# First chunk of x by DMA transpose, first product pair ahead of the parameters, exponentials on GpSimd, and a new order of products

## The chip, the cores and the metric

The kernel runs on one core of one Trainium2 chip. Its engines work side by side and meet through semaphores: TensorE (matrix products, PE in the profile), VectorE (DVE), ScalarE (ACT), GpSimd (POOL) and SyncE (SP), which here only issues DMA transfers. ScalarE can issue transfers too. The metric is the device time of one execution in microseconds, lower is better.

## What is computed

The reference mixes two branches of a token sequence x (2048 tokens, 448 columns, bfloat16) by a gate per token. Branch a is a state-space layer with 448 complex states, a recurrence over the tokens; branch b is a feed-forward layer with 1792 hidden columns.

```python
x = A_x
g = sigmoid((x * gate_w).sum(-1, keepdims=True))
# branch a
Lam = Lambda_re + 1j * Lambda_im
dt = exp(log_dt)
Lam_bar = exp(dt * Lam)
B_bar = ((Lam_bar - 1.0) / Lam)[:, None] * (B_re + 1j * B_im)
Bu = einsum("bld,pd->blp", x + 0j, B_bar)
h_t = Lam_bar * h_(t-1) + Bu_t            # for every token t
y = 2.0 * einsum("blp,dp->bld", h, C_re + 1j * C_im).real + x * Dskip
# branch b
b = silu(x @ w1) @ w2
out = g * y + (1 - g) * b
```

## The kernel before

The tokens are cut into 4 chunks of 512. For each chunk there are five kinds of work.

- *B products* (`bu`, line 635): x times the transposed B, seven slots of 128 rows (`BT`), into `U`. Slots 0 to 2 and half of slot 3 are the real part, the rest the imaginary part.
- *Lanes* (`lanes`, line 654): the complex recurrence is turned by cosine and sine tables (`COS`, `SIN`) into real scans. DVE does the turning, seven scans of 512 tokens (line 665), and the turning back into `H`. ScalarE or, for the slots named in `GP` (line 626), GpSimd casts each scan's result from `Gf` to `Gb`. Small GpSimd products carry the state to the next chunk (`k1`, `k2`, `gin`).
- *First FFN product* (`f1`, line 690): x times w1, 14 blocks of 128 hidden columns, evicted by ScalarE with Silu into `aT`.
- *Second FFN product* (`ffn2`, line 697) for each block of 128 tokens: 14 products with w2, evicted by ScalarE with the factor 1 − g into `Tb`.
- *Readout* (`readout`, line 717) for each block of 128 tokens: 7 products of `H` with `CP`, then a DVE instruction that adds the rest, then the store.

`bu` and `f1` need x transposed (`xT`: four column blocks, the last of them columns 320 to 447, of which the half not covered already counts). They are made in pairs by `step` (line 605): a pair is 14 "half steps", products over 64 rows that use the upper and the lower half of the array in turn, 8 that begin the pair and 6 that end it. A pair stays open until the next one has begun; `close` (line 621) ends it at once.

The head of the kernel. SP issues the x load of chunk 0, four B loads, ten w1 loads, the w2 load, and then DMA transposes of x for chunk 1 and of C. ScalarE issues four small parameter loads (`prm`) and loads the table for Exp. TensorE first runs 15 filler products on a zeroed tile (`idle`, line 420), then transposes chunk 0 of x in 16 pieces (`x_transposes`, line 432), the parameters (`prm_t`, line 485) and B slots 0 and 1 (`b_transposes`, line 458). DVE and ScalarE copy the results from PSUM to SBUF. From the transposed parameters `pc` (line 495) ScalarE makes `dtc` = exp(log_dt) and `rc` = exp(dt Re Lambda) (lines 500 and 504), and then loads the table that has Silu and Sin. DVE makes the phases for the tables from `dtc`. GpSimd makes `gwc`, the gate weights, from `pc`; `gates` (line 767) needs them.

The order of work. Each call of `add` puts an operation with its engine, estimated cost and priority into a `Plan`. `order` (line 102) runs a small model: TensorE keeps the order in which the operations were added (the calls at lines 800 to 868), the other queues take at each moment a ready operation with the lowest priority number, and PSUM banks are assigned on the way. What comes out is the fixed order of instructions of each engine. The estimated costs therefore influence the orders and the banks, and nothing else. `Waits` then puts in the semaphore waits.

Of the kernel before, what the change touches and what calls it, by code (L numbers as in the profile page):

```python
# [46 lines left out]
class Plan:  # L47
# [6 lines left out]
    SWITCH = 0.10  # L54

# [46 lines left out]
    def order(self):  # L102
# [28 lines left out]
        while len(done) < len(ops):  # L131
# [20 lines left out]
            if o.sem is not None:  # L152
                free[o.eng] = t + o.cost
                if o.bytes > 4096:
                    pipe = max(pipe, t + 1.5) + o.bytes / 260e3
                    o.end = pipe + 0.4
                else:
                    o.end = t + 3.4
            else:
# [4 lines left out]
                free[o.eng] = o.end = t + o.cost + extra  # L164
# [97 lines left out]
def bass_gated_mix__ssm_conv_s5__dense_activation_silu__prompt_kernel(nc, A_x, A_Lambda_re, A_Lambda_im, A_B_re, A_B_im, A_C_re, A_C_im,  # L262
               A_log_dt, A_Dskip, B_x, B_w1, B_w2, gate_w, out):
    with ExitStack() as ctx:
# [26 lines left out]
        Cnat = Tb[0:112, 13:15, :].rearrange("p a b -> p (a b)")[:, 0:768].rearrange("p (b l) -> p b l", b=4)  # L291
        gwc = sb("gwc", [128, 4], BF16)
# [13 lines left out]
        pc = sb("pc", [128, 4, 4], F32)  # L306
        dtc = sb("dtc", [128, 4], F32)
# [49 lines left out]


# [7 lines left out]
        def load_xt(tc, n, prio, cost, reads=()):  # L366

            rows = slice(tc * CH, (tc + n) * CH)
            for k, (o, c) in enumerate(((slice(0, 3), slice(0, 384)), (slice(3, 4), slice(320, 448)))):
                P.add("sp", lambda e, o=o, c=c: e.dma_start_transpose(xT[:, o, rows], x2[rows, c]), list(reads),  # L370
                      [f"xT{t}{k}" for t in range(tc, tc + n)], cost[k], prio + k, sem(), n * CH * (1100, 500)[k])

        load_x(0, 0)
        load("sp", Bnat[:, 0:3, :], A_B_re[0:384, :].rearrange("(s p) d -> p s d", p=128), "Bn0", 384 * 896, 1)
        load("sp", Bnat[:, 4:7, :], A_B_im[0:384, :].rearrange("(s p) d -> p s d", p=128), "Bn3", 384 * 896, 2)
        load("sp", Bnat[0:64, 3, :], A_B_re[384:448, :], "Bn1", 64 * 896, 3)
        load("sp", Bnat[64:128, 3, :], A_B_im[384:448, :], "Bn2", 64 * 896, 4)
        for h, (c0, c1) in enumerate(((0, 384), (384, 896))):
            w = w1s[:, :, :].rearrange("p b (q f) -> p b q f", q=2)
            for b in range(3):  # L380
                load("sp", w[:, b, :, c0:c1], B_w1[128 * b:128 * b + 128, :].rearrange("p (q f) -> p q f", q=2)[:, :, c0:c1],
                     f"w1{h}{b}", 128 * 4 * (c1 - c0), 5 + h)
            load("sp", w[64:128, 3, :, c0:c1], B_w1[384:448, :].rearrange("p (q f) -> p q f", q=2)[:, :, c0:c1],
                 f"w1{h}3", 64 * 4 * (c1 - c0), 5 + h)
            load("sp", w1s[0:64, 3, c0:c1], B_w1[320:384, c0:c1], f"w1{h}4", 64 * 2 * (c1 - c0), 5 + h)
# [11 lines left out]
        def late_loads():  # L397
# [4 lines left out]
            for tc in range(1, NCH):  # L402
# [12 lines left out]
        ACT(lambda e: e.preload_act_table(AF.Exp), [], ["tbl"], 1.3, 4)  # L415


        DVE(lambda e: e.memset(PB[:, 0, :], 0.0), [], ["PB0"], 0.2, 0)  # L418

        def idle(n):  # L420
# [6 lines left out]
            P.add("pe", mm, ["PB0"], [tk], 0.107 * n)  # L427

        idle(15)


        def x_transposes(h, n):

            tk = Ps()

            def mm(pe):
                for q in range(2):
                    for b in range(2):
                        o = (q * 2 + b) * 128
                        c = XCOL[2 * n + q]  # L440
                        r = pe.transpose(bk16(tk)[:, o:o + 128], xnat[:, 2 * h + b, c:c + 128], ident[:, :])  # L441
                return r
            P.add("pe", mm, ["xn0", "ident"], [tk], 0.24)
            dst = xT[:, 2 * n:2 * n + 2, 256 * h:256 * h + 256]
            src = lambda: bk16(tk)[:, 0:512].rearrange("p (q n) -> p q n", q=2)
            if n == 0:
                DVE(lambda e: e.tensor_copy(dst, src()), [tk], [f"xT00{h}"], 0.42, 0)
            else:
                ACT(lambda e: e.activation(dst, src(), AF.Copy), [tk], [f"xT01{h}"], act_cost(512), 0)

        for h in range(2):
            for n in range(2):
                x_transposes(h, n)

        def xr(tc):
            return [f"xT{tc}{k}" for k in (range(2) if tc else ("00", "01", "10", "11"))]

        def b_transposes(slots, reads, h, to_act):
# [11 lines left out]
            P.add("pe", mm, reads + ["ident"], [tk], 0.06 * 2 * n)  # L470
# [10 lines left out]

        prmn = [f"prm{k}" for k in range(4)]
# [9 lines left out]
        b_transposes(B01, ["Bn0"], 0, False)  # L492
        b_transposes(B01, ["Bn0"], 1, True)
        idle(2)
# [5 lines left out]
        ACT(lambda e: e.activation(dtc[:, :], LDT, AF.Exp), ["pc", "tbl"], ["dtc"], 0.25, 1)  # L500
# [3 lines left out]
        ACT(lambda e: e.activation(rc[:, :], rc[:, :], AF.Exp), ["rc", "tbl"], ["rc"], 0.25, 1)  # L504
        ACT(lambda e: e.preload_act_table_set("silu_and_others"), [], ["tbl", "dtc", "rc"], 1.3, 2)
# [48 lines left out]
        DVE(lambda e: e.tensor_single_scalar(ph[:, 4:8], ph[:, 0:4], 512.0, ALU.mult), ["ph"], ["ph5"], 0.2, 12)  # L554
        DVE(nearest(phk[:, 4:8], ph[:, 4:8]), ["ph5"], ["phk5"], 0.2, 12)
        DVE(minus(ph[:, 4:8], ph[:, 4:8], phk[:, 4:8]), ["ph5", "phk5"], ["ph5"], 0.2, 12)
        ACT(lambda e: e.activation(s8[:, :], ph[:, :], AF.Sin, scale=TURN), ["ph", "ph5", "tbl"], ["s8"], 0.25, 12)
        ACT(lambda e: e.activation(pha[:, :], ph[:, :], AF.Abs), ["ph", "ph5", "tbl"], ["pha"], 0.25, 12)
        ACT(lambda e: e.activation(c8[:, :], pha[:, :], AF.Sin, bias=hpi[:, :], scale=-TURN), ["pha", "hpi", "tbl"], ["c8"], 0.3, 12)
# [344 lines left out]
```

## Time and profile before

| what | us |
|---|---|
| three runs | 143.53, 144.14, 144.27; median 144.14 |
| the profiled execution | 143.92 |
| its span, from first to last instruction | 142.0 |
| TensorE busy | 137.6 (97%) |
| DVE busy | 126.1 (89%) |
| ScalarE busy | 79.1 (56%) |
| GpSimd busy | 34.2 (24%) |

The lines of the profile name a line of the code, an engine, an operation, the tile written and the tiles read (buffer numbers left out), and a count. A busy TensorE is not a TensorE at its peak, as matmuls are pipelined and the ends are modelled. The chain of waits is followed back from the last instruction: at each moment it shows the piece of work that the end waited for. L599 is the half steps, L703 the second FFN product, L731 the readout, L425 the filler, L441 the x transposes, L468 the B transposes, L774 the gates.

### The profile page before, as it was taken

What the parts mean: (1) busy time and instruction counts of PE and PEld (TensorE: products, weight loads), DVE (VectorE), ACT (ScalarE), POOL (GpSimd) and SP (SyncE); (2) the same over time, 40 slices, a digit from 0 to 9 for tenths busy, and PEclk for the clock granted to TensorE, in tenths of its full rate; (3) what the DMA queues carried; (4) which work ended last, traced back from release to release, by engine and by line L of the source; (5) the groups of instructions that cost most, each with busy time, mean ns of one, the idle gap of its engine ahead of it and who ended that gap; (6) DMA issues with size and microseconds to landing.
All of it is one profiled execution on the core that took longest, in us unless ns stands there. A gap on an engine that the chain in (4) does not pass through costs nothing.

```text
span 142.0 us, 2706 instructions
## 1 busy us (share of the span) xinstructions
PE 137.6 (97%) x1069; PEld 70.6 (50%) x1069; DVE 126.1 (89%) x145; ACT 79.1 (56%) x148; POOL 34.2 (24%) x66
## 2 busy tenths in 40 slices
PE   6989999999999999999999999999999999999993
PEld 4855555544444544444555554444455555555552
DVE  0399999998899299999999999999999999899393
ACT  3386698798965494889811014898721355411100
POOL 7184000089009520443450002542000000000000
PEclk9999999999999999999999999999999999999999
DMA  4989969201947600101000102000001021000113
GB/s 133 331 258 290 314 133 201 33 0 39 239 103 188 229 5 0 37 0 42 2 31 1 41 29 69 18 18 5 0 30 34 0 69 37 31 1 32 32 65 99
DMA packets 21108, 11.44 MB, mean 81 GB/s; under 512 B 11492, under 2 KB 21096, under 8 KB 21096
## 3 DMA queue, kind: packets, MB, share of 16 engines
q1 hardware_dynamic: 21088, 11.27, 30.5%
q8 instruction: 8, 0.13, 0.4%
q14 instruction: 4, 0.03, 0.1%
q10 hardware_dynamic: 8, 0.00, 0.0%
HBM read 6.25 MB, written 1.84 MB: 57 GB/s over the span
## 4 chain that ended last, share of the span: by engine, by line
PE 96%; DVE 1%; ACT 1%; POOL 1%; issue 0%
PE ps L599 45%; PE ps L703 30%; PE ps L731 15%; PE ps L425 2%; PE ps L441 1%; PE ps L774 1%; ACT BT L475 1%; PE ps L468 1%; POOL cw L562 0%; DVE ot L735 0%; PE ps L751 0%; DVE PB L418 0%; POOL gwc L497 0%; DVE pc L495 0%; DVE cw L570 0%
## 5 line engine op out<-in xcount | busy, mean ns | idle before, releaser
L599 PE MATMUL ps<-xT,w1s 64*128 64x512 bf16 x392 | 47.4, 376 | 0.0
L703 PE MATMUL ps<-w2s,aT 128*128 128x448 bf16 x224 | 44.7, 352 | 0.0
L692 ACT ACTIVATE aT<-ps 128x512 bf16<-128x512 f32 x56 | 30.0, 601 | 5.3 <-PE ps L599 5.2
L599 PEld LDWEIGHTS ps<-xT,w1s 64*128 64x128 bf16 x392 | 21.0, 94 | 22.7 <-issue 0.7
L703 PEld LDWEIGHTS ps<-w2s,aT 128*128 128x128 bf16 x224 | 21.7, 98 | 20.3 <-issue 0.4
L665 DVE TENSOR_TENSOR_SCAN Gf<-rc,gin,PA 128x512 f32<-128x512 f32 x21 | 26.8, 1322 | 0.0
L599 PE MATMUL ps<-xT,BT 64*128 64x512 bf16 x196 | 25.9, 376 | 0.7 <-DVE ph L511 0.6
L707 ACT ACTIVATE Tb<-ps,g 128x448 bf16<-128x448 f32 x16 | 10.1, 633 | 28.0 <-PE ps L703 21.4
L731 PE MATMUL ps<-CP,H 128*128 128x448 bf16 (+1 forms) x119 | 23.2, 341 | 0.0
L671 ACT ACTIVATE Gb<-Gf 128x512 bf16<-128x512 f32 x24 | 14.7, 630 | 8.4 <-DVE Gf L665 8.3
L599 PEld LDWEIGHTS ps<-xT,BT 64*128 64x128 bf16 x196 | 10.7, 94 | 12.1 <-DVE phk L508 0.8
L731 PEld LDWEIGHTS ps<-CP,H 128*128 128x128 bf16 x119 | 11.5, 98 | 9.8 <-issue 0.4
L633 ACT ACTIVATE U<-ps 128x512 bf16<-128x512 f32 x24 | 13.3, 592 | 2.2 <-PE ps L599 2.2
L735 DVE SCALAR_TENSOR_TENSOR ot<-ps,g,tf 128x448 bf16<-128x448 f32 (+1 forms) x17 | 11.1, 650 | 3.2 <-issue 2.2
L669 POOL CAST Gb<-Gf 128x512 bf16<-128x512 f32 x4 | 6.1, 1518 | 23.0 <-DVE Gf L665 23.0
L721 DVE SCALAR_TENSOR_TENSOR tf<-xnat,g,Tb 128x448 f32<-128x448 bf16 x16 | 10.6, 674 | 0.1
L652 DVE TENSOR_TENSOR PB<-Gb,SIN 128x1536 bf16<-128x1536 bf16 (+1 forms) x8 | 8.6, 1087 | 1.2 <-ACT Gb L671 1.1
L652 DVE TENSOR_TENSOR PB<-U,SIN 128x2048 bf16<-128x2048 bf16 (+1 forms) x8 | 8.6, 1080 | 0.0
L652 DVE TENSOR_TENSOR PA<-U,COS 128x3584 bf16<-128x3584 bf16 x4 | 8.1, 2020 | 0.2
L652 DVE TENSOR_TENSOR PA<-PA,PB 128x3584 bf16<-128x3584 bf16 x4 | 8.1, 2018 | 0.0
L652 DVE TENSOR_TENSOR H<-PA,PB 128x3584 bf16<-128x3584 bf16 x4 | 8.1, 2014 | 0.0
L652 DVE TENSOR_TENSOR PA<-Gb,COS 128x3584 bf16<-128x3584 bf16 x4 | 8.1, 2014 | 0.0
(97 smaller groups left out, 100.5 us busy)
## 6 DMA issues: line engine op xcount, KB each, us to landing
xnat<-in_A_x_dram SPq DMA_DIRECT2D x4, 448.0 KB, 6.1
out_dram<-ot SPq DMA_DIRECT2D x15, 112.0 KB, 1.7
w2s<-in_B_w_dram SPq DMA_DIRECT2D x1, 1568.0 KB, 9.3
w1s<-in_B_w_dram SPq DMA_DIRECT2D x3, 256.0 KB, 4.6
w1s<-in_B_w_dram SPq DMA_DIRECT2D x3, 192.0 KB, 4.3
Gb<-Gb SPq DMA_DIRECT2D x8, 64.0 KB, 1.9
U<-U SPq DMA_DIRECT2D x6, 64.0 KB, 2.0
Tb<-in_A_B_re_dram SPq DMA_DIRECT2D x1, 336.0 KB, 3.7
```

The lines of the kernel that those rows point to most:

```text
L599: r = pe.matmul(bk(tk), w[p0:p0 + 64, k, c0:c0 + 128], xT[p0:p0 + 64, k, xc:xc + CH], start=(start and i == 0), stop=(not start and i == 2))
L633: ACT(lambda e: e.activation(U[:, s, :], bk(tk), AF.Copy), [tk], [f"U{s}"], act_cost(512), 4)
L652: return DVE(lambda e: e.tensor_tensor(o, a, b, op), r, w, dve_cost(n, 2), prio)
L665: DVE(lambda e, s=s, b=b, init=init: e.tensor_tensor_scan(Gf[:, s, :], rc[:, b:b + 1].to_broadcast([128, CH]), PA[:, s, :], init, ALU.mult ...
L669: POOL(lambda e, s=s: e.tensor_copy(Gb[:, s, :], Gf[:, s, :]), [f"Gf{s}"], [f"Gb{s}"], 0.75, 8)
L671: ACT(lambda e, s=s: e.activation(Gb[:, s, :], Gf[:, s, :], AF.Copy), [f"Gf{s}"], [f"Gb{s}"], act_cost(512), 4)
L692: ACT(lambda e: e.activation(aT[tc % 2][:, fb, :], bk(tk), AF.Silu), [tk, "tbl"], [f"aT{tc % 2}_{fb}"], act_cost(512), 3)
L703: r = pe.matmul(bk(tk)[:, 0:D_MOD], aT[tc % 2][:, fb, o:o + 128], w2s[:, fb, :], start=(fb == 0), stop=(fb == NFB - 1))
L707: ACT(lambda e, tk=tk: e.activation(Tb[:, tb, :], bk(tk)[:, 0:D_MOD], AF.Copy, scale=g1[:, tb:tb + 1]), [tk, f"g1_{tc}"], [f"Tb{tb}"] + [f ...
L721: DVE(lambda e: e.scalar_tensor_tensor(tf[tb % 2][:, :], xnat[:, tb, :], g[:, tb:tb + 1], Tb[:, tb, :], ALU.mult, ALU.add), [f"xn{tc}", f" ...
L731: r = pe.matmul(bk(tk)[:, 0:n], Ht[:, s, o:o + 128], CP[:, s, c], start=(s == 0), stop=(s == NSLOT - 1))
L735: DVE(lambda e, tk=tk, c=c, n=n: e.scalar_tensor_tensor(ot[tb % 3][:, c], bk(tk)[:, 0:n], g[:, tb:tb + 1], tf[tb % 2][:, c], ALU.mult, ALU ...
```

## The change

- Chunk 0 of x: columns 0 to 383 come by a DMA transpose on SP's queue, into `xT`. The last column block, 320 to 447, is loaded as it is by ScalarE's queue into the new tile `xlast`, transposed by TensorE in 4 pieces (`xl_t`) and copied by one DVE instruction. The natural copy of chunk 0, needed only for the skip term, is loaded with the late loads, after the first chunk's lanes.
- B_re rows 0 to 255 are loaded by ScalarE's queue ahead of `xlast` and of the four parameter loads; rows 256 to 383 get a load of their own on SP. The w1 loads are 8 instead of 10.
- TensorE's head: 12 filler products instead of 15, B slots 0 and 1, `xl_t`, 2 filler products, the first pair of B products, and only then the parameters, B slots 4 to 6, the end of the first pair, the gates, and B slots 2 and 3.
- `dtc` and `rc` are made by GpSimd as e to a power, with a constant tile `ebase`; ScalarE loads only the table with Silu and Sin.
- The phases of the carried state (`s8`, `c8`) get a higher priority; some casts of `Gb` move to GpSimd (`GP`).
- The order of products of all chunks is changed; the planner has new constants for several operations.

The functions `half_steps`, `step`, `close`, `u_out`, `bu` and `swapped` are only moved ahead of the first pair.

```diff
+    OVERLAP = {"act": 0.10, "dve": 0.08}
...
-                free[o.eng] = o.end = t + o.cost + extra
+                o.end = t + o.cost + extra
+                free[o.eng] = o.end - self.OVERLAP.get(o.eng, 0.0)
...
-        load_x(0, 0)
-        load("sp", Bnat[:, 0:3, :], A_B_re[0:384, :].rearrange("(s p) d -> p s d", p=128), "Bn0", 384 * 896, 1)
+        load("act", Bnat[:, 0:2, :], A_B_re[0:256, :].rearrange("(s p) d -> p s d", p=128), "Bn0", 256 * 896, -1)
+        load("act", xlast[:, :, :], x2[0:CH, 320:448].rearrange("(b p) d -> p b d", p=128), "xl", CH * 256, -0.5)
+        P.add("sp", lambda e: e.dma_start_transpose(xT[:, 0:3, 0:CH], x2[0:CH, 0:384]), [], ["xT00"], 1.45, 0, sem(), CH * 768)
         load("sp", Bnat[:, 4:7, :], A_B_im[0:384, :].rearrange("(s p) d -> p s d", p=128), "Bn3", 384 * 896, 2)
+        load("sp", Bnat[:, 2, :], A_B_re[256:384, :], "Bn4", 128 * 896, 3)
...
+            for q in range(2):
+                c = slice(896 * q + c0, 896 * q + c1)
+                load("sp", w1s[:, 0:3, c], B_w1[0:384, c].rearrange("(b p) f -> p b f", p=128), f"w1{h}{q}", 384 * 2 * n, prio)
...
-            for tc in range(1, NCH):
+            for tc in range(NCH):
                 load_x(tc, 18 + tc, ["Gb7b"])
...
-        ACT(lambda e: e.preload_act_table(AF.Exp), [], ["tbl"], 1.3, 4)
+        ACT(lambda e: e.preload_act_table_set("silu_and_others"), [], ["tbl"], 1.3, 3.5)
+        POOL(lambda e: e.memset(ebase[:, :], math.e), [], ["ebase"], 0.1, 1)
...
-        DVE(lambda e: e.memset(PB[:, 0, :], 0.0), [], ["PB0"], 0.2, 0)
+        DVE(lambda e: e.memset(PB[:, 0, 0:256], 0.0), [], ["PB0"], 0.15, 0)
...
-        idle(15)
...
-        for h in range(2):
-            for n in range(2):
-                x_transposes(h, n)
+        idle(12, 0.213)
...
+        b_transposes(B01, ["Bn0"], 0, False)
+        b_transposes(B01, ["Bn0"], 1, False)
+        tk = Ps()
+
+        def xl_t(pe, tk=tk):
+            for b in range(4):
+                r = pe.transpose(bk16(tk)[:, 128 * b:128 * b + 128], xlast[:, b, :], ident[:, :])
+            return r
+        P.add("pe", xl_t, ["xl", "ident"], [tk], 0.44)
+        DVE(lambda e, tk=tk: e.tensor_copy(xT[:, 3, 0:CH], bk16(tk)[:, 0:512]), [tk], ["xT01"], 0.42, 0)
+        idle(2, 0.213)
+
+        step(bu(0, 0), bu(0, 1))
...
         P.add("pe", prm_t, prmn + ["ident"], [tk], 0.3)
-        b_transposes(B01, ["Bn0"], 0, False)
-        b_transposes(B01, ["Bn0"], 1, True)
-        idle(2)
+        b_transposes(B456, ["Bn3"], 0, False)
+        b_transposes(B456, ["Bn3"], 1, True)
...
-        ACT(lambda e: e.activation(dtc[:, :], LDT, AF.Exp), ["pc", "tbl"], ["dtc"], 0.25, 1)
+        POOL(lambda e: e.tensor_tensor(dtc[:, :], ebase[:, :], LDT, ALU.pow), ["pc", "ebase"], ["dtc"], 0.3, 0)
...
-        ACT(lambda e: e.activation(rc[:, :], rc[:, :], AF.Exp), ["rc", "tbl"], ["rc"], 0.25, 1)
-        ACT(lambda e: e.preload_act_table_set("silu_and_others"), [], ["tbl", "dtc", "rc"], 1.3, 2)
+        POOL(lambda e: e.tensor_tensor(rc[:, :], ebase[:, :], rc[:, :], ALU.pow), ["ebase"], ["rc"], 0.3, 0)
...
-        GP = ((), (0, 1), (0, 1), ())
+        GP = ((0, 1), (0, 1), (0, 1), (0,))
...
-        BU(0, (0, 1))
-        b_transposes(B456, ["Bn3"], 0, False)
-        b_transposes(B456, ["Bn3"], 1, True)
-        b_transposes(B23, ["Bn0", "Bn1", "Bn2"], 0, False)
-        b_transposes(B23, ["Bn0", "Bn1", "Bn2"], 1, True)
+        close()
         gates(0)
+        b_transposes(B23, ["Bn4", "Bn1", "Bn2"], 0, False)
+        b_transposes(B23, ["Bn4", "Bn1", "Bn2"], 1, True)
         BU(0, (4, 5), (6, 2))
         step(bu(0, 3), f1(0, 7))
-        F1(0, (0, 8), (1, 9), (2, 10), (3, 11), (4, 12), (5, 13))
+        F1(0, (4, 12), (1, 9), (3, 11), (0, 8), (5, 13))
         lanes(0)
         late_loads()
         skip(0)
+        F1(0, (2, 10))
...
-        BU(2, (0, 1), (4, 5), (6, 2))
+        BU(2, (6, 2))
         step(bu(2, 3), f1(2, 7))
-        F1(2, (0, 8), (1, 9), (2, 10), (3, 11), (4, 12), (5, 13))
+        F1(2, (0, 8), (1, 9), (4, 12), (5, 13))
         close()
         gates(2)
         gates(3)
         C(0)
+        F1(2, (2, 10), (3, 11))
         F2(4)
...
-        step(f1(3, 0), bu(3, 3))
-        BU(3, (0, 1), (4, 5), (6, 2))
-        F1(3, (1, 7), (2, 8), (3, 9), (4, 10), (5, 11), (6, 12))
+        BU(3, (0, 1))
+        F1(3, (3, 9), (2, 8))
+        BU(3, (6, 2))
+        F1(3, (1, 7), (4, 10), (5, 11), (6, 12))
...
+        C(8)
         lanes(3)
-        F2(12)
-        C(8)
-        F2(13)
+        F2(12, 13)
         C(9)
...
```

## The prediction

> **What bounds the kernel now.** I read the chain of waits in order of time first, because it says which engine sets the end at each moment.
>
> ```profile
> 7.90 1.02 PE ps L599 x8
> 8.92 0.79 PE ps L468 x12
> 9.71 0.02 issue
> 9.74 0.82 ACT BT L475
> 10.56 0.14 issue
> 10.69 18.95 PE ps L599 x174
> 29.64 2.75 PE ps L703 x14
> ...
> 71.04 2.65 PE ps L703 x14
> ...
> 132.89 6.65 PE ps L731 x42
> 139.54 0.02 issue
> 139.57 0.45 DVE ot L735
> ```
>
> The columns are start, length and what. From 10.69 to 139.54 us the chain holds nothing but TensorE pieces: 128.85 us without a gap. So a faster DVE, ScalarE or GpSimd instruction after 10.69 buys nothing, and the only places where this change can gain are the 10.69 us ahead of the dense part and the two microseconds of the tail. The tail (last DVE piece, then the store) is untouched. So I next read the timeline of TensorE up to 11 us.
>
> ```profile
> 1.18 3.38 PE L425 MATMUL ps<-PB 128*128 128x256 bf16 x15 [1.18 <-DVE PB L418]
> 4.35 1.91 PE L441 MATMUL ps<-ident,xnat 128*128 128x128 bf16 x16
> 6.49 0.62 PE L468 MATMUL ps<-ident,Tb 128*128 128x128 bf16 x8
> 6.94 0.38 PE L425 MATMUL ps<-PB 128*128 128x256 bf16 x2
> 7.88 1.04 PE L599 MATMUL ps<-xT,BT 64*128 64x512 bf16 x8 [0.56 <-DVE ph L511]
> ```
>
> Two things are to be seen. The first real product starts at 7.9 us, 0.6 us after TensorE ran dry. And TensorE is slow at first although the granted clock reads 1.00 in every slice: 16 transposes of x take 1.91 us, 0.119 each, while 12 transposes of B at 8.92 take 0.79 us, some 0.06 each. The slow stretch runs from 1.18 to about 6.2 us, 5.0 us.
>
> **The sum is worked out for T1, the moment the first pair of B products starts.** What TensorE must do between T1 and the start of today's dense part, in the new order, at the full pace:
> - first pair, 8 half steps: at the dense 18.95/174 = 0.109 us each, 0.87;
> - a change from half-height to full-height products: 0.10 (the first group of 14 on L703 after half steps took 2.75, one after a readout 2.65);
> - the parameter transposes: 0.31 (6.27 to 6.57 today, between two chain pieces);
> - 20 transposes of B: today's 12 took 0.79 with a change of height in it, so 0.0575 each, 1.15;
> - another change of height, 0.10, because the pair is now closed before the gates (its six half steps are already inside the 128.85);
> - 16 gate products: a group of 32 took 0.89 with a change, so 0.40.
>
> Sum 2.93 us. One more change of height appears later, since two FFN pairs now stand behind the first readout: 0.10. The rest of the new order has the same products, so the end of TensorE moves from 10.69 + 128.85 to T1 + 3.03 + 128.85, and the gain is 7.66 − T1.
>
> **T1, path by path.** Three things have to be there.
>
> ```profile
> xnat<-in_A_x_dram SPq DMA_DIRECT2D x1, 448.0 KB, 3.4
> Tb<-in_A_B_re_dram SPq DMA_DIRECT2D x1, 336.0 KB, 3.7
> Tb<-in_A_B_im_dram SPq DMA_DIRECT2D x1, 336.0 KB, 4.7
> Tb<-in_A_C_re_dram SPq DMA_TRANSPOSE x1, 4.4
> ```
>
> The last column is us from issue to landing. (a) The first 256 rows of B_re (224 KB), now first on ScalarE's queue at 0.72, where the first parameter load stood: at 3.4 to 4.7 it lands at 4.1 to 5.4. TensorE's filler, 12 instead of 15 products at 0.225 each (2.7 us, from 1.05), ends at 3.75, so it waits some 0.4 us. Then 8 slow transposes, 0.95, to 5.1 (to 6.35 late). (b) The last 128 columns of x (128 KB, issued at 1.27) land at 4.7 to 6.0 by the same rows; 4 slow transposes, 0.48, end at 5.55; the DVE copy of 512 columns is 0.42 and two hand-overs are 0.1: 6.1. The two B copies on DVE, 0.42 each, are done by then. (c) Columns 0 to 383 by DMA transpose, issued at 0.73: the C transpose of 336 KB took 4.4, the one of 768 KB for two chunks 6.6. 384 KB therefore land at 5.1 to 7.3; on the straight line between the two rows at 4.6, so 5.3, plus some 0.4 for sharing the engines with (a) and (b), 5.7. I take T1 = 6.2, path (b) and one more hand-over, with 5.6 (the clock quick before 6 us) and 7.4 (late landings) as ends.
>
> The DMA engines already run at 300 GB/s and more from 2.5 us on. The Trainium skill speaks against (b) here: "DMA: Bandwidth & Descriptors", section "Why small descriptors are slow (HBM only)", counts 27% overhead for a 256-byte descriptor, which is what a row of 128 columns is. By it (b) would take some 0.1 us more at the present rate, an estimate; no row of this trace isolates such a load.
>
> **The other edits.** The DMA queue of SP: the transpose holds it 1.5 us (half of the 3.08 of two chunks) where the x load held 0.5, the B loads are four as before, w1 goes in 8 issues instead of 10 at 0.65 each, so its last issue comes at about 9.2 against 9.4. B_im lands at 2.3 + 4.7 = 7.0; it is wanted at T1 + 1.3 = 7.5. The second part of w1 is wanted earlier, because the second FFN pair is now (4, 12): at T1, 2.93 for the head, and 6 + 8 + 14 + 14 half steps at 0.109, 4.6, so 13.7; by the slowest w1 landing in the table of DMA issues, 4.9, it is there at 14.1, by the 4.4 of the last today at 13.6. So 0 to 0.4 us of wait; I take 0. The exponentials on GpSimd: the first stands between pc and everything phased, and the gate weights queue behind it on GpSimd. Rows of 128x4 there run from 0.19 to 1.22 us, one small copy took 2.03. The gates come 1.1 us after pc, so up to about 0.7 is hidden; DVE's copies near it are small, like those beside the 0.20 rows, so I take 0.3, cost 0. ScalarE loses two Exp and one table load (1.28 us); it was waiting for TensorE anyway (the 0.82 chain piece is a copy that began right after its transposes), so this is worth 0. The phases and so the first scan come about 0.7 us later on DVE. The cover is DVE's lead at the end: H of the last chunk is finished at 130.08 and first read at about 134.2, 4.1 us. With TensorE 1.5 earlier and DVE 0.7 later 1.9 of it is left; without it, each microsecond of DVE would be one of the end. More Gb casts on GpSimd (1.52 us against 0.63) sit under seven scans of 1.2 us each, also 0. The x load of chunk 0 moves behind the late loads: wanted by a DVE product at 64.8, issued near 43: 0. The planner's own changed constants only decide orders.
>
> **Sum.** Gain 7.66 − 6.2 = 1.46 us. The profiled execution took 143.92 (span 142.0 and 1.9 around it), so 142.46 there; the median of the runs shown is 144.14, 0.22 above it, so **142.7 us**. With T1 at 5.6 and 7.4 it is 142.1 and 143.9.
>
> **Rivals.**
> - *The clock stays low.* If TensorE's idle 0.4 us near 4 and the bits before T1 start the 5.0 us slow stretch anew at 4.1, it ends at 9.1, and the 2.9 us from T1 run at half pace: 1.45 us lost, 144.15. For it: work is thinner before 6 us than now. Against: today's gap of 0.56 us at 7.3 did not bring it back. The Trainium skill, "TensorE: Matmul & The Clock Gate", Part 1, says full speed follows one busy window of about 3.4 us that runs freely. By it a gap can cost a whole window, up to 1.7 us, an estimate; our 5.0 us would be a part window and a whole one.
> - *The transpose arrives late.* At 7.3 or beyond (the 768 KB row, or the sharing with two ScalarE loads weighs more): T1 = 7.5 to 8, 144.0 to 144.5. For it: today's chunk 1 transpose took 10.1 us, but behind a 1568 KB load. Against: here it is the first on its queue.
> - *GpSimd's power is slow, and the kernel slower than before.* One mechanism: the power takes 2.0 us and the gate weights behind it 1.2, as the slow GpSimd rows; then the gates on TensorE wait 2.0 + 1.2 + 0.1 − 1.1 = 2.2 us, 0.74 more than the gain, 144.9. It decides from 2.6 us for the power, the copy and the fill behind it together (the 1.1 hidden and the 1.46 gained). For it: no power is in the trace; against: rows beside small DVE work are 0.2.
> - *More than forecast*: the clock comes up before the transposes, T1 = 5.6 or below: 141.8 to 142.1.
>
> **Chances.** Forecast (142.2 to 143.4): 0.50. Better: 0.10. Low clock: 0.14. Late transpose: 0.13. Slow power or another wait of that size: 0.13. A measurement of this kernel tells about 0.5%, 0.7 us, from no change. The first two cases and a little of the next two are faster by over that, 0.62; the low clock and late transpose mostly within it, 0.24; the rest slower, 0.14. The range reaches from the best case to the upper end of the late one, 141.8 to 144.5.
>
> **What would show it.** In the new trace the first half steps should start at 6.0 to 6.5, at 0.13 us each or less; the chain should be TensorE alone from there; the gates should show no wait for GpSimd; and (4, 12) none for w1. A first half step at 0.21 us means the low clock; an idle TensorE up to 7.3 means the transpose; a hole ahead of the gates means the power. Wrong altogether would be a new hole behind 14 us, where I expect none: a wait for H, for a full PSUM bank or for ScalarE in the reordered part.

## The result and the profile after

| | kernel before | changed kernel |
|---|---|---|
| median of 11 executions each, us | 143.94 | 146.01 |
| lowest to highest, us | 143.07 to 144.47, and one of 164.31 | 144.87 to 148.04 |
| profiled execution, us | 143.92 | 144.87 |
| its span, us | 142.0 | 142.7 |

The change makes the kernel slower: the ratio to the kernel before is 1.011 (95% interval 1.008 to 1.015). This ratio leaves disturbed executions out, so it lies below the ratio of the two medians. The executions fall into two heaps, five from 144.87 to 145.31 and six from 146.01 to 148.04. The profiled one belongs to the first heap, so its 0.95 us over the profiled execution before is one question and the second heap another.

The chain of waits of the changed kernel, in order of time (start, length, what):

```profile
1.19 4.11 DMA xlast<-in_A_x_dram
...
6.35 1.04 PE ps L480 x8
...
7.71 0.18 DVE pc L557
7.89 0.08 issue
7.97 1.05 POOL dtc L562
9.04 0.16 DVE ph L563
...
19.45 0.72 ACT SIN L603
20.17 0.49 ACT aT L697
20.67 0.04 issue
20.71 7.78 PE ps L480 x70
28.49 2.75 PE ps L708 x14
31.25 12.84 PE ps L480 x118
...
53.75 8.87 DVE Gf L670 x7
...
63.18 0.59 ACT U L511
63.77 0.05 issue
63.81 2.33 PE ps L480 x20
```

Before, everything from 10.69 us on was TensorE. Now the end hangs on a path that leaves TensorE at 7.7 us with the parameters (`pc`), goes through GpSimd's power, DVE's phases and ScalarE's SIN, and comes back to TensorE at 20.71, and on a second path through DVE's scans (L670) and ScalarE that comes back at 63.81.

TensorE's own timeline (start, length, instructions, in brackets the idle time before them and what ended it):

```profile
5.34 0.40 PE L535 MATMUL ps<-ident,xlast 128*128 128x128 bf16 x4 [0.70 <-DMA xlast<-in_A_x_dram]
5.57 0.38 PE L440 MATMUL ps<-PB 128*128 128x256 bf16 x2
6.35 1.04 PE L480 MATMUL ps<-xT,BT 64*128 64x512 bf16 x8 [0.39 <-DVE xT L538]
7.32 0.22 PE L549 MATMUL ps<-ident,prm 4*128 4x4 bf16 x3
...
9.40 0.55 PE L779 MATMUL ps<-gwc,xT 128*128 128x1 bf16 x16 [0.20 <-POOL gwc L560]
...
10.35 0.82 PE L480 MATMUL ps<-xT,BT 64*128 64x512 bf16 x6
```

The first pair does start at 6.35, 1.5 us earlier than before. What becomes of this lead:

| up to | what it took beyond the forecast, us | lead left, us |
|---|---|---|
| 6.35, the first pair (T1) | 0.15 (6.35 against 6.2) | 1.31 (7.66 − 6.35) |
| 10.35, dense half steps | 0.42: 4.00 from T1 against 2.93 + 0.65 for the end of the first pair | 0.89 |
| 28.49, second FFN product | 0.50: 162 half steps at 0.109 are 17.64, they took 18.14 | 0.39 |
| 66.14, gates of chunks 2 and 3 | 0.84 hole (TensorE idle) at 63.0, the forecast change of height apart | −0.45 |
| 140.11, the end of TensorE | 0.12 in small pieces | −0.57 (139.54 before) |

(At 28.49 the old kernel stood at 29.64, but with one pair more closed, 0.65; the difference then is 0.50, of which the change of height that comes later takes 0.10.) From 102.9 us to the end the two kernels take the same 37.2 us. The store after that adds 0.1 to the span, and what lies outside the span was 2.17 against 1.92, which varies by 0.2 between executions of the kernel before, too.

ScalarE's timeline ahead of the hole in chunk 2:

```profile
59.98 0.63 ACT L676 ACTIVATE Gb<-Gf 128x512 bf16<-128x512 f32 x1 [0.57 <-DVE Gf L670]
60.52 0.58 ACT L511 ACTIVATE U<-ps 128x512 bf16<-128x512 f32 x1
61.47 0.63 ACT L676 ACTIVATE Gb<-Gf 128x512 bf16<-128x512 f32 x1 [0.37 <-DVE Gf L670]
62.00 0.58 ACT L697 ACTIVATE aT<-ps 128x512 bf16<-128x512 f32 x1
62.64 0.63 ACT L676 ACTIVATE Gb<-Gf 128x512 bf16<-128x512 f32 x1
63.18 0.58 ACT L511 ACTIVATE U<-ps 128x512 bf16<-128x512 f32 x1
```

ScalarE works strictly in its written order. Its casts (L676) wait for DVE's scans, and the eviction of `U` at 63.18, whose PSUM bank TensorE needs, stands behind the last of them. The change also gives these casts priority 1 where they had 4, one of the planner's new constants.

### The profile page after: what moved, and what is told of

Its sections match the earlier page's. It is cut to its first block, busy times and chain, and to the rows that moved or that the text cites. A ratio compares the mean times of both kernels' runs of the same rounds, so it can differ in the third digit from the quotient of the medians.

```text
span 142.7 us, 2670 instructions
## 1 busy us (share of the span) xinstructions
PE 136.8 (96%) x1054; PEld 67.9 (48%) x1054; DVE 125.9 (88%) x145; ACT 74.9 (52%) x139; POOL 44.4 (31%) x72
## 4 chain that ended last, share of the span: by engine, by line
PE 74%; DVE 17%; DMA 3%; issue 3%; ACT 1%; POOL 1%; ACTq 0%; DVEq 0%
PE ps L480 31%; PE ps L708 26%; PE ps L736 15%; DVE Gf L670 6%; DMA xlast<-in_A_x_dram 3%; DVE U L509 2%; DVE PB L657 1%; DVE Gf L587 1%; PE ps L779 1%; DVE CP L766 1%; DVE Gf L605 1%; POOL dtc L562 1%; DVE PA L657 1%; DVE Gf L572 1%; DVE Gf L569 1%
## 5 line engine op out<-in xcount | busy, mean ns | idle before, releaser
L480 PE MATMUL ps<-xT,w1s 64*128 64x512 bf16 x392 | 48.2, 376 | 0.9 <-ACT U L511 0.8
L480 PE MATMUL ps<-xT,BT 64*128 64x512 bf16 x196 | 26.7, 377 | 0.4 <-DVE xT L538 0.4
L670 DVE TENSOR_TENSOR_SCAN Gf<-rc,gin,PA 128x512 f32<-128x512 f32 x21 | 26.6, 1311 | 0.0
L674 POOL CAST Gb<-Gf 128x512 bf16<-128x512 f32 x7 | 10.2, 1456 | 46.9 <-DVE Gf L670 46.9
L676 ACT ACTIVATE Gb<-Gf 128x512 bf16<-128x512 f32 x21 | 13.2, 630 | 18.2 <-DVE Gf L670 18.0
L670 DVE TENSOR_TENSOR_SCAN Gf<-rc,PA 128x512 f32<-128x512 f32 x7 | 8.6, 1259 | 0.0
```

The lines of the kernel that those rows point to most:

```text
L480: r = pe.matmul(bk(tk), w[p0:p0 + 64, k, c0:c0 + 128], xT[p0:p0 + 64, k, xc:xc + CH], start=(start and i == 0), stop=(not start and i == 2))
L670: DVE(lambda e, s=s, b=b, init=init: e.tensor_tensor_scan(Gf[:, s, :], rc[:, b:b + 1].to_broadcast([128, CH]), PA[:, s, :], init, ALU.mult ...
L674: POOL(lambda e, s=s: e.tensor_copy(Gb[:, s, :], Gf[:, s, :]), [f"Gf{s}"], [f"Gb{s}"], 1.5, 8)
L676: ACT(lambda e, s=s: e.activation(Gb[:, s, :], Gf[:, s, :], AF.Copy), [f"Gf{s}"], [f"Gb{s}"], act_cost(512), 1)
```

## The experiments

After the comparison the candidates were: the power on GpSimd (1.04 us instead of the 0.3 forecast); the new order of products with ScalarE's casts; a quick clock that comes late, for the second heap; and the place of the parameters, which now stand behind the first pair, on the path to all phases. Each run below is timed beside the kernel before (medians 143.55 to 143.9).

**The power.** In the first run both powers are replaced by a multiplication and an addition, so the numbers computed are others and both exponentials are left out. In the second only the planner is told their real cost.

```diff
-POOL(lambda e: e.tensor_tensor(dtc[:, :], ebase[:, :], LDT, ALU.pow), ["pc", "ebase"], ["dtc"], 0.3, 0)
+POOL(lambda e: e.tensor_single_scalar(dtc[:, :], LDT, -0.07, ALU.mult), ["pc", "ebase"], ["dtc"], 0.3, 0)   # e1, rc alike
+POOL(lambda e: e.tensor_tensor(dtc[:, :], ebase[:, :], LDT, ALU.pow), ["pc", "ebase"], ["dtc"], 1.05, 0)     # e9, rc alike
```

> The changed kernel with both powers on GpSimd replaced by one multiplication and one addition of the same shape (dt becomes -0.07 times log_dt, and the decay 1 plus its exponent; the exponentials are left out). All engines keep their order. Theory A (the power of 1.04 us delays the gates and, through DVE, the scans, so that the scans come 2 us later than ScalarE's fixed order allows for): the wait at the gates is gone, DVE's chain is 0.75 us earlier, the hole of 0.84 us on TensorE at 63 us shrinks to 0.2 or less, and the span is 141.2 to 141.9 (changed kernel 142.7). Theory B (the ScalarE casts of Gb at priority 1 stand in front of the PSUM evictions, whatever the power does): the hole stays at 0.6 or more and the span is 142.0 to 142.5. Theory C (the new order of products is at fault): the same as B.

> The changed kernel with the planner told 1.05 us for each power instead of 0.3; the operations are the same, only the fixed orders differ. Theory A, in the part that says that the mismatch between plan and chip is what costs in chunk 2: ScalarE's order puts the PSUM evictions of chunk 2 ahead of the late casts, the hole at 63 us shrinks to 0.3 or less, the head stays as it is, span 141.9 to 142.3. Rival (the delay itself costs, whatever the order): hole of 0.6 or more, span 142.5 to 143.0.

Measured: 146.31 (ratio 1.010 to 1.025, single executions in both heaps, from 145.27 to 147.20) and 147.13 (1.015 to 1.028). Without the power the gates wait for nothing, but the hole in chunk 2 is there, 0.8 us as before, and one of 0.9 for `aT` at 20.7. From the first pair to the dense half steps it takes 3.73 us instead of 4.00, so 0.27 of the 0.42 in the table is the power's; it is not the cause of the rest. In e9 the hole in chunk 2 shrinks to 0.24, as expected, but TensorE waits 0.69 us for w1 before 15.29 and 0.81 for `aT` before 22.32.

**The clock.** Three kernels: the order of products as before (e3); more filler, so that TensorE isn't idle ahead of the first pair (e4); and e4 with the parameter transposes ahead of the first pair (e10).

```diff
+        idle(3, 0.213)     # e4, between the B transposes and xl_t
-        idle(2, 0.213)
+        idle(4, 0.107)     # e4, ahead of the first pair
```

> The changed kernel with the order of products of the kernel before, from the pair (4, 5) of chunk 0 on; head, loads, powers and casts stay new. Theory A: the head still loses 0.9 us against the forecast, but ScalarE's order in chunk 2 has U3 ahead of two of the casts, so the hole at 63 us is 0.3 or less and the one extra change of height is gone: span 141.6 to 142.1. Theory C (the new order alone costs): 141.0 to 141.5, with the early loss gone too. Theory B: hole of 0.6 or more, span 142.4 to 142.8.

> The changed kernel with three more filler products between the B transposes and the transposes of the last x columns, and four instead of two behind these, so that TensorE has no gap of more than 0.2 us before the first pair. Theory D (the runs of 146 to 148 us are executions in which TensorE's quick clock comes later, because of the gaps of 0.70 and 0.39 us before the first pair): all runs lie within 1 us of the fastest, at 144.7 to 145.5, median 145.0. Rival (the spread has another source): half of the runs lie again above 146. Neither expects a gain in the quickest run of more than 0.3 us.

> The run with filler (e4, span 143.3, first pair at 6.85), with the parameter transposes ahead of the first pair again. Theory E (DVE has 16.3 us of work without a pause between the parameters and the first product of the lanes, before and after the change; the first pair ahead of the parameters starts this work 1.1 us later, and ScalarE's and TensorE's waits behind it cost what was gained): pc comes 0.9 us or more earlier, the first lanes product (24.5 in e4) comes at 23.8 or earlier, the wait of TensorE for ScalarE near 20 us is gone, the hole in chunk 2 is smaller by the same 0.7 or so, and the span is 142.2 or less although the first pair starts 0.1 to 0.3 later. Rival (DVE's start does not matter, the order of products or the plan does): 143.0 to 143.6.

Measured: e3 146.69 (1.005 to 1.019, single executions from 144.99 to 147.37), e4 145.31 (1.007 to 1.014, all four from 145.20 to 145.39), e10 147.19 (1.021 to 1.027). The profiled execution of e3 is one of the slower heap, 147.37, and shows what that heap is. TensorE's timeline there:

```profile
6.71 1.89 PE L480 MATMUL ps<-xT,BT 64*128 64x512 bf16 x8 [0.18 <-DVE xT L538]
...
8.84 1.46 PE L460 MATMUL ps<-ident,Tb 128*128 128x128 bf16 x12
10.24 0.87 PE L480 MATMUL ps<-xT,BT 64*128 64x512 bf16 x6
```

The first pair takes 1.89 instead of 1.04, twelve transposes 1.46 instead of 0.84; the six half steps after them are quick again. The late quick clock thus costs 1.47 us on these two groups alone, though the granted clock reads 1.00 in every slice. In e4, with filler, the heap is gone. But filler does not always prevent it: in e10's profiled execution the first pair took 1.89, too, and its four executions lie within 0.2 us of each other, so it says nothing on the parameters.

**The order of products and the planner.** e14 is e4 with the order of before; e15 is e4 without the planner's new `OVERLAP`; e16 is e10 without it; f22 is e16 with the phases of the carried state back at their old priority.

```diff
-    OVERLAP = {"act": 0.10, "dve": 0.08}
+    OVERLAP = {}                                                  # e15, e16, f22
-            ["s8"], 0.25, 2)
+            ["s8"], 0.25, 12)                                     # f22; ph5, phk5, pha, c8 alike
```

> The run with filler (e4) with the order of products of the kernel before from the pair (4, 5) of chunk 0 on. Theory E: the order decides only where DVE's lateness meets TensorE; the span stays at 142.8 to 143.6, with the hole at another place. Theory C (the new order costs by itself): 141.5 to 142.3.

> The run with filler (e4) with the planner's new constant OVERLAP taken out, so that the plan sees DVE and ScalarE later by 0.08 and 0.10 us for each instruction; same operations, other fixed orders. Theory F (in chunk 2 ScalarE's fixed order puts the cast of the last scan ahead of a PSUM eviction, because the plan has the scans 2 us too early): now two or three casts stand behind that eviction, the hole of 0.84 us in chunk 2 is 0.3 or less, span 142.2 to 142.8 if no new hole comes. Rival (the order of ScalarE is not what holds): hole stays, 143.1 to 143.6.

> e10 and e15 together. Theories E and F: both holes gone, span 141.0 to 141.8, below the kernel before (142.0). If only E holds, as e10; if only F, as e15.

> The changed kernel with filler, parameters ahead of the first pair and no overlap in the planner (145.38 when it ran), and the angles for the readout (ph5, s8, c8) back at their old priority of 12, so that ct and CP are made later. If ct and CP standing ahead of the aT evictions made the 0.9 us hole before the first product of the second feed-forward, it goes: span 141.6 to 142.2, median 143.6 to 144.3. If a fixed queue only meets the late DVE in another place, a new hole of 0.5 to 1.0 us stands between 20 and 70 us and the median stays at 144.8 to 145.6.

Measured: e14 144.93 (1.005 to 1.012), e15 145.52 (1.008 to 1.016), e16 145.38 (1.007 to 1.014), f22 147.75 (1.022 to 1.034). In e15 and e16 the hole in chunk 2 is gone, and another is there. What TensorE waited for in e16 (total, times, longest):

```profile
PE ps L709 <- ACT aT L698: 0.9, 1, 0.9
PE ps L480 <- ACT aT L698: 0.3, 1, 0.3
```

So the 0.84 us hole is a matter of ScalarE's order, but another order only meets a late DVE somewhere else. The attempt to remove that one, f22, missed altogether: one wait of 2.7 us for `aT`, in an execution that was at half clock around 9 us besides (see the last section).

**The head alone.** f20 has the changed head (with filler), and behind it everything as before: order, casts, constants. f23 gives both exponentials back to ScalarE, f24 also puts the parameters ahead of the first pair, f21 has the parameters first and the powers on GpSimd.

```diff
-GP = ((0, 1), (0, 1), (0, 1), (0,))
+GP = ((), (0, 1), (0, 1), ())                     # f20; priorities, costs and the order of products as before, too
...
-        step(bu(0, 0), bu(0, 1))
         P.add("pe", prm_t, prmn + ["ident"], [tk], 0.3)
+        step(bu(0, 0), bu(0, 1))                  # f24, f21
```

> The changed head (loads, xlast over TensorE, first pair ahead of the parameters, powers on GpSimd, and enough filler to bring the clock up) with everything behind it as in the kernel before: its product order, its GpSimd share of the Gb casts, its planner constants. If the loss came from the other edits (new order, more casts on GpSimd, new constants), only the head is left and it gains: TensorE without a hole behind the first feed-forward product, span 141.0 to 141.5, median 142.7 to 143.2. If the loss comes from the DVE queue, which starts 1.1 us later because pc stands behind the first pair, it loses again although nothing behind the head differs: first half step at 6.4 to 6.8, holes of 0.3 to 1.5 us in which TensorE waits for ScalarE's aT or U behind work of DVE, span 142.5 to 143.5, median 144.4 to 145.4.

> As the run of the head alone, with both powers given back to ScalarE as Exp (two activations and two table loads as before). If the power of 1.05 us on GpSimd is a share of the loss, the phases come 0.8 to 1.6 us earlier on DVE (two powers against two Exp of 0.2 to 0.3), the gates wait 0.2 instead of 0.9, and the span is 0.3 to 1.0 below that of the head alone. If not (the table load of 1.28 us in ScalarE's queue ahead of SIN takes its place), the two spans agree within 0.3.

> As the one before, with the parameter transposes ahead of the first pair, as in the kernel before: DVE's parameter copy at 5.5 to 6.8 as in the kernel before (6.6), the phases no later than there. If the late start of DVE's queue is what costs, this one has none of it and keeps what is left of the head: median 143.0 to 143.6, below the kernel before by 0.3 to 0.9. If the head gains nothing on its own (DVE's queue of 16 us between the parameters and the first phased product sets the pace whatever TensorE does), the median is 143.7 to 144.5 and the first product of the second feed-forward waits for aT.

> The head alone with the parameters ahead of the first pair, but with the powers on GpSimd: the fourth of a square of which three have run (pair first with powers 145.33, pair first with Exp 145.64, parameters first with Exp 144.34). If the place of the parameters is what counts and the power is not, it stands by the one with Exp: 144.0 to 144.8, span 141.8 to 142.4. If the power is what counts once the parameters are early, 145.0 to 145.8, with GpSimd's power in the chain of waits and the gates waiting for gwc.

Measured: f20 145.33 (1.009 to 1.015), f23 145.64 (1.010 to 1.016), f24 144.34 (1.004 to 1.010), f21 146.12 (1.012 to 1.019). The head alone loses as much as e4, the whole change with the same filler (145.31): the new order, the casts and the constants are not needed for the loss. As its expectation had it for a late DVE, TensorE waits in f20 for `aT` (0.37 us, before 23.92) and for DVE's `CP` (1.16, before 58.22). Giving back the exponentials changes nothing that can be measured: the gates no longer wait, but the table load of 1.28 us now stands ahead of `th`, a step of the gates, in ScalarE's queue, and TensorE waits 0.80 us for that. Putting the parameters first gains 1.3 us in the median. f21, meant as the fourth corner, fell to the late clock (first pair 1.89; one execution of its six stood at 144.93) and tells nothing.

f24 is still 0.4 to 1.0% slower than the kernel before, though its first pair starts 0.83 us earlier (7.05 against 7.88). Its profiled span, 142.0, is that of the kernel before, and its chain shows where the lead went:

```profile
19.57 2.11 ACT COS L607 x2
21.68 0.98 ACT aT L698 x2
...
22.71 6.87 PE ps L479 x62
29.57 2.75 PE ps L709 x14
```

From 16.38 to 22.66 the end hangs on ScalarE, whose evictions of `aT` have SIN and COS between them. The last COS ends at 21.68, in the kernel before at 21.60, and the second FFN product begins at 29.57, there at 29.64. The phases come no earlier in f24 either (7.29 against 7.26). This fits the second branch of its expectation, that DVE's work from the parameters on sets the pace up to there whatever TensorE does; the wait for `aT` came a little earlier than it had it, 0.32 us before 22.71.

**The parameters alone.** Both kernels are the kernel before with one thing moved. g1 puts the parameter transposes behind the transposes of B and the filler; h1 puts them behind the first pair.

```diff
-        P.add("pe", prm_t, prmn + ["ident"], [tk], 0.3)   # g1: ahead of the B transposes
         b_transposes(B01, ["Bn0"], 0, False)
         b_transposes(B01, ["Bn0"], 1, True)
         idle(2)
+        step(bu(0, 0), bu(0, 1))                          # h1 only; was first in the order of products
+        P.add("pe", prm_t, prmn + ["ident"], [tk], 0.3)
```

> The kernel before with one line moved: its parameter transposes behind the eight transposes of B_re and the two filler products, so pc comes 0.6 to 1.0 us later and the first pair of B products 0.3 us earlier. If DVE's queue from pc on is what sets the pace up to 30 us, the first phased product (PA) follows pc by 16.3 us as everywhere so far, at 23.6 to 24.1 instead of 22.98, TensorE meets it as new waits for aT or U, and the span grows by 0.3 to 1.0 (142.3 to 143.0, median 144.0 to 144.8). If TensorE sets the pace alone, as the prediction had it, the span falls by 0.3 (141.7).

> The kernel before with one thing of the change alone: its first pair of B products stands ahead of the parameter transposes (x still over TensorE, exponentials on ScalarE, order, casts and constants as they were). The pair can start about 0.3 us earlier, and pc comes behind it, at 8.1 to 8.8 instead of 6.59. If the late parameters are what ate the gain, this kernel is slower by 0.7 to 1.6 us: gates waiting 0.5 or more for gwc, new waits for aT or U between 15 and 60 us, span 142.7 to 143.6, median 144.6 to 145.5. If the parameters have cover, as the prediction took it, it is 0 to 0.3 faster (span 141.7 to 142.0).

Measured: g1 143.79 (0.996 to 1.003), h1 144.55 (1.004 to 1.010), just under its range for late parameters; its gates did not wait. g1's expectation failed, because in its profiled execution the quick clock came 1.1 us earlier than in that of the kernel before, so its parameters were not late. But this makes it the twin that h1 needs. In h1's profiled execution the clock came as early; both start the first pair within 0.2 us of each other and the dense half steps at the same moment, and only the parameters differ. g1, the chain, then a line of ScalarE's and one of DVE's timeline:

```profile
9.68 18.95 PE ps L599 x174
28.63 2.75 PE ps L703 x14
```

```profile
19.52 1.16 ACT L545 ACTIVATE COS<-Gf,hpi 128x1024 bf16<-128x1024 f32 x1
```

```profile
6.49 0.17 DVE L495 CAST pc<-ps 128x16 f32<-128x16 bf16 x1 [0.30 <-PE ps L489]
...
21.72 2.03 DVE L652 TENSOR_TENSOR PA<-U,COS 128x3584 bf16<-128x3584 bf16 x1
```

h1, the same views:

```profile
9.71 6.23 PE ps L485 x56
...
21.63 1.03 ACT COS L599
22.66 0.50 ACT aT L694
...
23.21 6.86 PE ps L485 x62
30.07 2.75 PE ps L705 x14
```

```profile
21.50 1.17 ACT L599 ACTIVATE COS<-Gf,hpi 128x1024 bf16<-128x1024 f32 x1
22.54 2.08 ACT L694 ACTIVATE aT<-ps 128x512 bf16<-128x512 f32 x4
```

```profile
7.99 0.17 DVE L549 CAST pc<-ps 128x16 f32<-128x16 bf16 x1 [1.90 <-PE ps L546]
...
24.10 2.02 DVE L654 TENSOR_TENSOR PA<-U,COS 128x3584 bf16<-128x3584 bf16 x1
```

The parameters are 1.50 us later, the last COS 1.98, `PA` 2.38, and the second FFN product begins 1.44 us later, at 30.07 instead of 28.63, because ScalarE's SIN and COS, which wait for DVE's phases, stand between the evictions of `aT`: TensorE waits 1.23 us for `aT` before 23.21. The end (last `ot`) is 1.07 us later, 139.99 against 138.92. (The planner orders the other queues anew in h1; that is part of the difference.)

**Relief for DVE.** If DVE were the pace, taking evictions of B products off it should help. g5 is e14 and g6 is e4 with U5, the eviction of slot 5 of `U`, given to ScalarE, g8 is e14 with U5 and U6.

```diff
-                u_out(s, tk, tc == 0 and s in (1, 2, 5, 6))
+                u_out(s, tk, tc == 0 and s in (1, 2, 6))      # g5, g6; (1, 2) in g8
```

> The changed kernel with filler and the old order of products (144.93 when it ran), with one of DVE's four evictions of B products in chunk 0 (U5, 0.60 us) given to ScalarE. If DVE's queue is the pace, PA comes 0.6 us earlier after pc (15.7 instead of 16.3) and the span falls by 0.3 to 0.6, to 142.2 to 142.5, median 144.2 to 144.6. If ScalarE's queue is the pace, it grows by 0.2 to 0.6.

> The changed kernel with filler (145.31 when it ran, span 143.3) and its own new order, U5 given to ScalarE. If the hole of 0.84 us in chunk 2 comes from DVE being late, 0.6 us less on DVE takes 0.4 to 0.6 off it: span 142.7 to 142.9, median 144.7 to 144.9. If it is ScalarE's order alone, the hole stays at 0.8 and the span at 143.3.

> As the one before, with two evictions (U5 and U6) given to ScalarE. If DVE's queue is the pace, PA follows pc by 15.1 us and the span is 141.7 to 142.2, at or below that of the kernel before; if ScalarE's evictions are then what comes late, new waits for aT of 0.5 us and more stand before the second feed-forward and the span is 142.8 or more.

Measured: 146.83 (1.016 to 1.025), 146.68 (1.013 to 1.023), 148.06 (1.023 to 1.033). `PA` does follow `pc` by 15.8, 15.8 and 15.3 us, instead of 16.3 in the changed kernel and 16.4 in the kernel before, near what was expected; the time was expected to fall and rises by 1.4 to 3.1 over e14 and e4. What TensorE waited for in g8:

```profile
PE ps L480 <- ACT aT L698: 1.8, 3, 0.9
PE ps L709 <- ACT aT L698: 1.6, 1, 1.6
```

In g5, with U5 alone on ScalarE, the waits are 1.2 for `aT` and 1.0 for `U`. Half a microsecond to one less on DVE comes back as more than that on ScalarE. So DVE is not the pace by itself: its lateness counts where it reaches ScalarE's queue. What else came late in these three plans was not followed further.

No version tried beats the kernel before; g1, at no measurable difference, comes nearest.

## Why the prediction was wrong, by its own steps

- **T1** was right: 6.35 against 6.2, on path (b) as chosen. `xlast` took 4.1 us from issue to landing, inside the 3.4 to 4.7. The transpose was not late, w1 was not waited for, and the tail did not move.
- **The exponentials on GpSimd**, "I take 0.3, cost 0": one power takes 1.04 us, so the gates waited. That is 0.27 of the 0.42 by which the head behind T1 exceeded the sum: without the power, in e1 and f23, this stretch takes 3.73 instead of 4.00. The mechanism was named by the rival and only its size was off: 1.04 between the 0.3 taken and the rival's 2.0. The rest stands in the two groups of B transposes that half steps follow, 0.78 and 0.54 from start to start where the sum has 0.69 and 0.46: it counts the change from half height to full height, not the way back.
- **"The phases and so the first scan come about 0.7 us later on DVE. The cover is DVE's lead at the end"** is the step that failed. The phases (`ph`) came 1.78 us later, at 9.04. In the kernel before:

```profile
6.59 0.17 DVE L495 CAST pc<-ps 128x16 f32<-128x16 bf16 x1 [0.29 <-PE ps L489]
...
7.26 0.15 DVE L501 SCALAR_TENSOR_TENSOR ph<-dtc,pc 128x4 f32<-128x4 f32 x1
```

  Of this, 1.12 is `pc`, moved behind the first pair (7.71 against 6.59), and 0.66 the power. The prediction does not say what its 0.7 is made of; its own terms put `pc` alone 0.9 later (6.2 + 0.87 + 0.10 + 0.31 = 7.48). Worse, the cover was looked for at the end of the kernel, 100 us away. The consumers stand at 13 to 23 us, where DVE's own busy time leaves no room. The windows of the kernel before (stretch, length, then PE, PE's weight loads, DVE, ACT, POOL busy, the clock, DMA share, GB/s):

```profile
11.00:20.00 9.00, 9.00 (x88) 4.68 (x86) 8.91 (x17) 6.46 (x13) 1.29 (x3) 1.00 1.11 256
20.00:30.00 10.00, 10.00 (x93) 5.08 (x90) 9.93 (x11) 8.49 (x17) 1.23 (x2) 1.00 0.54 104
```

  DVE is busy for 18.84 of these 19 us, and the table functions on ScalarE wait for it in the middle of the evictions. A late DVE is covered there by nothing but TensorE's own order, and h1 shows what it costs: 1.4 us at the second FFN product for 1.5 us of parameters, against g1. This was in the profile of before; the 89% of the whole span hid it.
- **"A faster DVE, ScalarE or GpSimd instruction after 10.69 buys nothing"** describes the chain of the kernel before (no run made one of these faster and nothing else), and tempted to the converse, that a slower or later one costs nothing. A chain that is TensorE alone says that the others were in time, not by how much. Nor does a gain ahead of 10.69 come through by itself: f24's 0.83 us were down to 0.07 at the second FFN product.
- **New order, casts on GpSimd, "has the same products"**, costed at 0.10 and 0: a hole of 0.84 us in chunk 2 appears with them, and goes with another plan (e15, e16). But the head alone loses as much without them (f20), so they say where the lateness shows, not that it does.
- **The rival of the low clock** came true in about half of the executions. Its price for slow products was right, 1.45 forecast, 1.47 in e3's two groups. In the whole time it costs more: e3's executions of 147.3 lie 2.3 above its quickest, and in its profile the parameters come at 8.96 instead of 7.71, too. Its chance, 0.14, was too low: the 0.4 us of idle foreseen at 4 did not come, but 0.70 ahead of the `xlast` transposes and 0.39 behind them did. The five executions of the first heap have a median of 144.91, 0.97 over the kernel before: that is the loss without the low clock. The step from there to 146.01 is put down to the clock by e3 and e4; no profile of the changed kernel itself shows its second heap.
- The text's own sign of being "wrong altogether", a new hole behind 14 us from ScalarE in the reordered part, is what was found.

What stays open: how much of the 0.50 up to 28.49 belongs to the power and how much to the parameters' place in the changed kernel itself, since the fourth corner fell to the clock; what part of each difference is the planner's, which orders the other queues anew in nearly every version; and why f24's executions, of which three in ten lie above 145, have a higher median than the kernel before although the profiled spans agree.

## What to carry to other kernels

When work is moved on the busiest engine, follow what is moved behind it to its first consumer, and read the other engines' busy share in that stretch, not over the whole span or at the end. Where each engine runs a fixed order, an instruction that comes late holds up everything written behind it, and a new order only moves the place where that shows. Idle gaps of a few tenths of a microsecond in the head can, in part of the executions, cost more than the work saved there, through the clock.

## What the runs showed of the hardware that was not expected

- The moment at which TensorE becomes quick differs between executions with the same work up to it. In h1 sixteen x transposes, from 4.20 on, took 1.06 us; in the kernel before, with the same instructions up to there, 1.91, and TensorE was quick only from about 6.2; in e3 it was still slow at 9. The granted clock reads 1.00 throughout in these three. The Trainium skill, "TensorE: Matmul & The Clock Gate", Part 1, puts the change after one busy window of about 3.4 us that runs freely, and the moment within half a microsecond from run to run, though a note in the same part has one kernel with 6, 11 or 14 slow products. A window missed by the idle time would account for e3's delay, and that the filler of e4 removes it speaks for this; e10 and f21, slow with filler, show that it is not the whole of it. The half microsecond is not what the runs show: some 2 us lie between h1 and the kernel before.
- The quick clock can also be lost again, and this the profile does show. In f22 eight B transposes (0.71 us from 3.63) and the four of `xlast` (0.40 from 5.51) were quick already; after waits of 0.84 and 1.07 us for loads the first pair at 7.78 took 1.89, and the granted clock reads 0.50 from 7.5 to 10.5. Over that execution it is 0.988 in the mean, and so it is in two of the six executions in the changed kernel's second heap; the other four read 1.00, like e3.
- A power on GpSimd takes 1.04 us for 128x4 numbers, where a multiplication by a constant on the same shape takes 0.24 (e1).
- The same DVE instruction can take very different times beside GpSimd. In e1 `Gf` took 0.48 and 0.92 us, both times while a GpSimd product of 512 columns ran (from 9.77 for 1.59, and from 11.82 for 2.24):

```profile
10.41 0.48 DVE L584 TENSOR_SCALAR Gf<-itf,ph 128x512 f32<-128x512 f32 x1
...
12.35 0.92 DVE L584 TENSOR_SCALAR Gf<-itf,ph 128x512 f32<-128x512 f32 x1
```

  The Trainium skill, "SBUF — State Buffer", section "SBUF: two separate sides", has GpSimd and a DVE instruction in a two-port mode, or with two SBUF inputs, lock a shared port pair for a whole instruction, the loser blocked. The trace does not say in which mode this one ran, and GpSimd's spans are rough. As they stand, neither was blocked: DVE's first ended at 10.89, before GpSimd's at 11.36, its second at 13.27, before GpSimd's at 14.06. What made the second slower is not shown.
